# One more w1 block among the first transfers of a fused attention, soft MoE and FFN kernel

## The chip, the cores and the metric

The kernel runs on one core of one Trainium2 chip. The metric is the device time of one execution in microseconds (us), as a median of several runs; lower is better. One execution was also profiled.

## The reference

Three layers follow each other. All inputs and outputs are float32.

- Chunked attention over 4 batches, 8 heads, 768 positions and 64 dimensions: each chunk of 32 queries sees its own 32 keys, 16 to the left, 8 to the right and 8 memory keys.
- A soft mixture of experts on the 3072 tokens of width 512: 8 experts with 4 slots each. The logits `x @ phi` give one softmax over the tokens, which mixes the tokens into 32 slots, and one over the slots, which mixes the results back; between them each expert does `relu(slots @ w1[e]) @ w2[e]` with a hidden width of 1024.
- A feed-forward layer with a squared relu: `h = x @ w_in`, `g = s * relu(h)**2 + b`, `g @ w_out`, with a hidden width of 2048.

```python
x = attention(q, k, v, mem_k, mem_v)            # (3072, 512)
logits = x @ phi
d = softmax(logits, axis=0); slots = d.T @ x
slot_out[e] = relu(slots[e] @ w1[e]) @ w2[e]    # for 8 experts
x = softmax(logits, axis=1) @ slot_out
r = relu(x @ w_in); out = (s * r * r + b) @ w_out
```

## The kernel before

**The attention stage** works in 32 units. A unit is one pair of heads and one half (384 positions) of one batch. Four units make a group, of which there are eight; the group's tokens then go through the logits and the running softmax of the mixture. The loop at L488 is a software pipeline written out by hand: iteration s spreads K of unit s+1 on POOL (`kspread`), computes the scores of unit s on PE (`emit_s`, L291), does the softmax of unit s on DVE and ACT, transposes the probabilities of unit s-1 (`emit_t`, L323), multiplies those of unit s-2 by V (`emit_pv`, L331) and transposes the result of unit s-3 (`emit_xt`, L345). Steps of a finished group come in between.

**The transfers** are all issued on SP's queue, in the order of the program, and SP waits at each issue until its target buffer is free. `load_qk` (L246) brings Q and K of one unit, 396 KB, into one of five buffers. `load_v` (L256) brings V of two units, four transfers of 192 KB, into one of two buffers; it does so for even units only. `load_w(n)` (L189) brings the next n blocks of one list of weights: 16 blocks of w1, two of w_in, 16 of w2, then the rest. A block of w1 is 1 MB. A counter, `wnext`, remembers how far the list is; an argument `cap` makes a call do nothing once the counter has reached it. The first 15 blocks of w1 have places of their own, which nothing in the attention stage uses, so their issues wait for no engine. The sixteenth goes where attention had its keys, and later blocks go where keys, V or used blocks of w1 were.

Ahead of the loop a first set of transfers is issued (L457 to L465): K of unit 0, constants, K of units 1 and 2, one w1 block, V of units 0 and 1, K of unit 3, V of units 2 and 3, K of unit 4. In the loop each iteration s issues K of unit s+5 and, where s+1 is even and s is at least 3, V of units s+1 and s+2; every odd iteration ends with one w block, up to `NWA` = 15:

```python
            when(s + NKB, load_qk)
            if s >= 3:
                when(s + 1, load_v)
            if s % 2 == 1:
                load_w(1, NWA)
            if s == NU - 2:
                load_w(1)
        load_w(19 - wnext[0])
```

So the loop brings the fifteenth block in iteration 27, the sixteenth in iteration 30, and the call behind it three more.

**After attention** come eight steps with w1 (`emit_w1`, L655), sixteen with w2 (`emit_w2`, L696), and then the feed-forward layer (L881, L965, L977), whose weights come as halves of blocks (L203) as buffers come free. The last block of w2 is brought in three pieces (L212).

Of the kernel before, what the change touches and what calls it, by code (L numbers as in the profile page):

```python
# [34 lines left out]
def kernel(  # L35
# [54 lines left out]
    def area(pos, *shape, p=128):  # L90
        n = 1
        for d in shape:
            n *= d
        at, size, tile_ = next(x for x in segs if x[0] <= pos < x[0] + x[1])
        assert pos + n <= at + size
        a = tile_[0:p, pos - at:pos - at + n]
        if len(shape) == 2:
            a = a.rearrange("p (a b) -> p a b", a=shape[0])
        elif len(shape) == 3:
            a = a.rearrange("p (a b c) -> p a b c", a=shape[0], b=shape[1])  # L100
        return a
# [15 lines left out]
    with tc.manual_schedule():  # L117
# [71 lines left out]
        def load_w(n, cap=None):  # L189
            for _ in range(n):  # L190
                i = wnext[0]
                if i < (len(order) if cap is None else cap):
                    src = srcs[order[i][0]][order[i][1]]
                    p = at_[order[i]]
                    if p is SPLIT:
                        wt[order[i]] = [area(x, SLOT // 2) for x in p]
                        for x in range(2):
                            nc.sync.dma_start(out=wt[order[i]][x], in_=src[:, SLOT // 2 * x:SLOT // 2 * (x + 1)])
                        wnext[0] += 1
                        continue  # L200
                    if i >= npre:
                        t = area(p, SLOT // 2).bitcast(I32)
                        nc.sync.dma_start(out=t, in_=src.bitcast(I32)[:, SLOT // 2 * order[i][2]:SLOT // 2 * (order[i][2] + 1)])  # L203
                        wt[order[i]] = t
                        wnext[0] += 1
                        continue
                    t = area(p, SLOT)
                    if order[i] == ("w2", W2 - 1):
                        wt[order[i]] = [t[:, SLOT // 2 * x:SLOT // 2 * (x + 1)] for x in range(2)]
                        for x, w in ((0, 2), (2, 1), (3, 1)):  # L210
                            at = slice(SLOT // 4 * x, SLOT // 4 * (x + w))
                            nc.sync.dma_start(out=t[:, at], in_=src[:, at])  # L212
                        wnext[0] += 1
                        continue
                    if src.dtype != F32:
                        t, src = t.bitcast(I32), src.bitcast(I32)
                    nc.sync.dma_start(out=t, in_=src)
                    wt[order[i]] = t
                    wnext[0] += 1
# [19 lines left out]
        def unit(u):  # L239
            g, hp = divmod(u, NHP)  # L240
            b, hf = divmod(g, HALF)
            return g, b, hf, hp

        def load_qk(u):
            g, b, hf, hp = unit(u)
            nc.sync.dma_start(out=kbuf[(u + 3) % NKB][:, PAD:], in_=kq[b, hf, hp])  # L246

        def load_v(u):
            g, b, hf, hp = unit(u)
            if u % 2:  # L250
                return
            for h in range(2):
                for a in range(2):
                    r0 = 0 if a else LC - RC
                    src = vm[b, 2 * hp + h:2 * hp + 4:2, r0:r0 + CH, hf * NCU + a:hf * NCU + a + NCU, :]
                    nc.sync.dma_start(out=vbuf[u // 2 % 2][2 * h + a:128:4, :, h], in_=src.rearrange("x r c d -> r x (c d)"))  # L256
# [204 lines left out]
        load_w(1)  # L461
        load_v(0)
        load_qk(3)
        load_v(2)
        load_qk(4)  # L465

# [725 lines left out]
```

## Time and profile before

| what | us |
|---|---|
| median of 3 runs | 460.74 (460.23 to 462.44) |
| the profiled execution | 460.34 |
| its span, first to last instruction | 458.6 |
| PE busy in the span | 442.1 (96%) |
| ACT, DVE busy | 297.1 (65%), 283.9 (62%) |
| POOL busy | 84.8 (18%) |
| bytes by DMA | 83.03 MB, mean 181 GB/s |

PE is the TensorE matmul engine, DVE is VectorE, ACT is ScalarE, POOL is GpSimd and SP (SyncE) issues the transfers. A line such as L331 is a line of the kernel. Busy time of PE is modelled from pipelined matmuls, so a busy PE is not PE at its peak. The profile names who ended a wait from the semaphores' events.

### The profile page before, as it was taken

How to read it: one execution, taken by the hardware profiler on the slowest of the kernel's cores; microseconds unless marked ns; L12 is line 12 of the kernel's file. 1: busy time of each engine (PE TensorE's matmuls, PEld its weight loads, DVE VectorE, ACT ScalarE, POOL GpSimd, SP SyncE). 2: the span in 40 equal slices, each digit the busy share in tenths (PEclk: the TensorE clock that was granted, in tenths of full speed). 3: DMA queues.
4: the chain of work that ended last, by engine and by line, in shares of the span. 5: the costliest groups of instructions: out<-in, count | busy, mean ns of one | idle time of the engine just before them, and what ended most of it. 6: DMA issues, size and time to landing. Idle time of an engine off the chain costs nothing.

```text
span 458.6 us, 10105 instructions
## 1 busy us (share of the span) xinstructions
PE 442.1 (96%) x3936; PEld 339.8 (74%) x3936; DVE 283.9 (62%) x644; ACT 297.1 (65%) x588; POOL 84.8 (18%) x155
## 2 busy tenths in 40 slices
PE   6899999999999989999999999999999999999996
PEld 5666766667556468788787888888888888888885
DVE  5678888788674089698695958994722242224242
ACT  4566666666325199889797987666666666664660
POOL 6575555561000000000000000000870000000000
PEclk8899999999999999999999999999999999999999
DMA  8999999999999953245252100000500020002011
GB/s 305 370 407 409 403 407 406 400 391 377 417 417 418 407 212 105 94 138 185 91 187 90 46 1 0 1 1 0 218 13 1 1 91 1 0 2 91 0 70 69
DMA packets 22735, 83.03 MB, mean 181 GB/s; under 512 B 2976, under 2 KB 3104, under 8 KB 18592
## 3 DMA queue, kind: packets, MB, share of 16 engines
q1 hardware_dynamic: 22688, 82.39, 46.8%
q8 instruction: 31, 0.51, 0.5%
q14 instruction: 16, 0.13, 0.1%
HBM read 76.09 MB, written 6.29 MB: 180 GB/s over the span
## 4 chain that ended last, share of the span: by engine, by line
PE 80%; DMA 10%; DVE 4%; SPq 1%; issue 1%; ACT 1%; POOL 1%; DVEq 0%; POOLq 0%; ACTq 0%
PE g L965 13%; PE pt L965 6%; PE xt L965 6%; PE x L965 6%; PE lp L965 6%; PE g L977 6%; DMA vals<-in_vm_dram 6%; PE s L881 5%; PE lp L977 3%; PE xt L977 3%; PE pt L977 3%; PE x L977 3%; PE s L655 3%; PE x L331 3%; DMA keys<-in_w_out_dram 2%; PE s L291 2%
## 5 line engine op out<-in xcount | busy, mean ns | idle before, releaser
L916 DVE TENSOR_TENSOR glo<-keys,ghi 128x512 fp32r<-128x512 f32 x48 | 35.8, 751 | 60.0 <-ACT ghi L912 59.8
L904 ACT ACTIVATE keys<-s 128x512 f32<-128x512 f32 x48 | 28.7, 598 | 44.9 <-PE s L881 44.9
L916 DVE TENSOR_TENSOR glo<-r,ghi 128x384 fp32r<-128x384 f32 x64 | 35.3, 554 | 16.9 <-ACT ghi L912 16.6
L948 POOL TENSOR_TENSOR vals<-vals,bias 128x512 f32<-128x512 f32 x7 | 10.3, 1487 | 168.4 <-ACT keys L904 168.4
L307 ACT ACTIVATE seg<-seg 128x384 f32<-128x384 f32 x32 | 28.8, 901 | 18.2 <-DVE seg L318 14.8
L904 ACT ACTIVATE r<-s 128x384 f32<-128x384 f32 x64 | 31.1, 488 | 13.7 <-PE s L881 13.5
L977 PE MATMUL g<-wlo,ghi 128*128 128x512 f32 x128 | 39.6, 389 | 0.0
L965 PE MATMUL g<-whi,ghi 128*128 128x512 f32 x126 | 39.3, 390 | 0.0
L965 PE MATMUL g<-whi,glo 128*128 128x512 f32 x126 | 39.1, 389 | 0.0
L908 ACT ACTIVATE r<-r 128x384 f32<-128x384 f32 x63 | 33.2, 526 | 6.5 <-DVE glo L916 4.7
L881 PE MATMUL s<-cpack,mpack 128*128 128x384 f32 (+1 forms) x112 | 36.3, 360 | 0.0
L268 POOL TENSOR_SCALAR keys<-keys 64x416 f32<-64x416 f32 x63 | 33.6, 533 | 12.5 <-DMA keys<-in_kq_dram 7.7
L291 PE MATMUL s<-keys 128*32 128x128 f32 x768 | 29.6, 286 | 4.9 <-POOL keys L272 3.8
L912 ACT CAST ghi<-r 128x384 fp32r<-128x384 f32 x64 | 32.5, 508 | 1.9 <-PE g L977 0.4
L908 ACT ACTIVATE keys<-keys 128x512 f32<-128x512 f32 x48 | 30.4, 633 | 1.8 <-DVE glo L916 0.2
L331 PE MATMUL x<-vals,seg 128*32 128x128 f32 x744 | 28.9, 280 | 2.7 <-DMA vals<-in_vm_dram 2.4
L912 ACT CAST ghi<-keys 128x512 fp32r<-128x512 f32 x48 | 29.8, 621 | 1.6
L331 PEld LDWEIGHTS x<-vals,seg 128*32 128x32 f32 x744 | 21.0, 111 | 12.7 <-DVE seg L315 5.3
L325 ACT COPY seg<-pt 128x384 f32<-128x384 f32 x32 | 15.2, 476 | 19.4 <-PE pt L323 18.5
L977 PEld LDWEIGHTS g<-wlo,ghi 128*128 128x128 f32 x128 | 24.0, 188 | 5.0
L965 PEld LDWEIGHTS g<-whi,glo 128*128 128x128 f32 x126 | 23.7, 188 | 5.0
L291 PEld LDWEIGHTS s<-keys 128*32 128x32 f32 x768 | 19.1, 112 | 10.8 <-POOL keys L272 6.6
(291 smaller groups left out, 1052.2 us busy)
## 6 DMA issues: line engine op xcount, KB each, us to landing
seg<-in_w_dram SPq DMA_DIRECT2D x27, 1024.0 KB, 8.8
keys<-in_kq_dram SPq DMA_DIRECT2D x32, 396.0 KB, 7.4
vals<-in_vm_dram SPq DMA_DIRECT2D x64, 192.0 KB, 6.6
keys<-in_w_out_dram SPq DMA_DIRECT2D x16, 512.0 KB, 4.5
keys<-in_w_in_dram SPq DMA_DIRECT2D x10, 512.0 KB, 3.9
out_dram<-seg SPq DMA_DIRECT2D x18, 256.0 KB, 2.1
keys<-in_w_in_dram SPq DMA_DIRECT2D x2, 1024.0 KB, 8.1
vals<-in_w_dram SPq DMA_DIRECT2D x2, 1024.0 KB, 10.2
```

Of the source, the lines that this page charges most:

```text
L268: (nc.vector if h and u == 0 else nc.gpsimd).tensor_scalar(out=stream(kz[rows, h], 0, CH), in0=k[rows, UT * h:UT * h + (NCU + 1) * CH].rea ...
L291: nc.tensor.matmul(out=o, lhsT=qt[:, 32 * c:32 * c + 32], rhs=kz[:, :, at:at + WIN], start=True, stop=not (first or last))
L307: nc.scalar.activation(out=p_r[u], in_=sm_r[u].rearrange("p t h (a r) -> p t r (h a)", a=2), func=AF.Exp, scale=scale)
L325: nc.scalar.copy(out=pts_r[u], in_=pt)
L331: nc.tensor.matmul(out=xp[32 * r:32 * r + 32, t], lhsT=pts_r[u][:, 32 * c:32 * c + 32], rhs=vbuf[u // 2 % 2][:, u % 2, :, 64 * c:64 * c + ...
L881: nc.tensor.matmul(out=hq, lhsT=mpack[:, 128 * f:128 * f + 128], rhs=cpack[:, 128 * t0:128 * (t0 + nt)], start=True, stop=True)
L904: nc.scalar.activation(out=r_of(n), in_=h_t.pop(n), func=AF.Relu)
L908: nc.scalar.activation(out=r2_of(n), in_=r_of(n), func=AF.Square)
L912: nc.scalar.copy(out=g_of(n)[0], in_=r2_of(n))
L916: nc.vector.tensor_tensor(out=glo, in0=r2_of(n), in1=ghi.bitcast(F32), op=ALU.subtract)
L965: nc.tensor.matmul(out=o_t[r_][t], lhsT=g[x][:, 128 * t:128 * t + 128], rhs=w_hi[f], start=(first and x == 0), stop=False)
L977: nc.tensor.matmul(out=o, lhsT=ghi[:, 128 * t:128 * t + 128], rhs=w_lo[f], start=False, stop=(f == f1 - 1))
```

## The change

One call is added among the first transfers: the second block of w1 is issued after K of unit 3 and ahead of V of units 2 and 3.

```diff
@@ -461,6 +461,7 @@
         load_w(1)
         load_v(0)
         load_qk(3)
+        load_w(1)
         load_v(2)
         load_qk(4)
 
```

## Rows read from the trace of the kernel before

**Rows 1.** The page: the span, and the DMA engines' share in 40 slices, in tenths.
```profile
span 458.6 us, 10105 instructions
...
DMA  8999999999999953245252100000500020002011
```

**Rows 2.** Stretches: length, busy us (instructions) of PE, PEld, DVE, ACT, POOL; PEclk, DMA share, GB/s.
```profile
20.00:100.00 80.00, 76.39 (x1507) 52.98 (x1498) 65.93 (x196) 51.49 (x110) 50.46 (x108) 1.00 1.02 404
100.00:112.00 12.00, 11.80 (x245) 9.06 (x240) 10.54 (x35) 8.16 (x19) 2.97 (x7) 1.00 0.98 367
112.00:162.00 50.00, 48.20 (x688) 28.32 (x676) 22.66 (x70) 18.60 (x61) 1.25 (x4) 1.00 1.01 415
```

**Rows 3.** PE's groups by line, 20 to 100 us: count | busy, mean ns | idle before.
```profile
L331 PE MATMUL x<-vals,seg 128*32 128x128 f32 x594 | 22.4, 275 | 2.7 <-DMA vals<-in_vm_dram 2.4 <-DVE seg L315 0.2
```

**Rows 4.** PE's timeline, end of w2: start, us, what, count, [idle before <- releaser].
```profile
148.32 2.80 PE L696 MATMUL pt<-seg,seg 128*32 128x256 f32 x48
151.39 1.07 PE L696 MATMUL xt<-seg,seg 128*32 128x256 f32 x16 [0.28 <-DMA seg<-in_w_dram]
...
156.75 2.83 PE L696 MATMUL xt<-seg,seg 128*32 128x256 f32 x32
```

**Rows 5.** SP's issues, one by one: K of units 3, 4; V of unit 4 (last); w.
```profile
6.75 0.59 SPq L246 DMA_DIRECT2D keys<-in_kq_dram  x1
...
11.58 0.58 SPq L246 DMA_DIRECT2D keys<-in_kq_dram  x1
...
19.82 0.61 SPq L256 DMA_DIRECT2D vals<-in_vm_dram  x1
...
20.47 0.59 SPq L217 DMA_DIRECT2D seg<-in_w_dram  x1
```

**Rows 6.** SP's waits: total, times, longest; 0 to 15 us, then 102 to 106.
```profile
SPq L256 <- DMA seg<-in_w_dram: 1.6, 1, 1.6
...
SPq L256 <- PE g L439: 2.9, 1, 2.9
```

**Rows 7.** DMA issues of rows 5, same order: KB, us from issue to landing.
```profile
keys<-in_kq_dram SPq DMA_DIRECT2D x1, 396.0 KB, 6.5
...
keys<-in_kq_dram SPq DMA_DIRECT2D x1, 396.0 KB, 5.6
...
vals<-in_vm_dram SPq DMA_DIRECT2D x1, 192.0 KB, 6.8
...
seg<-in_w_dram SPq DMA_DIRECT2D x1, 1024.0 KB, 8.6
```

**Rows 8.** Stretches of 1 us, columns as in rows 2: 13 to 15 us.
```profile
13.00:14.00 1.00, 1.00 (x11) 0.63 (x11) 0.99 (x3) 0.02 (x1) 0.53 (x1) 0.50 0.90 291
14.00:15.00 1.00, 1.00 (x24) 0.87 (x24) 0.71 (x4) 0.75 (x2) 0.89 (x2) 0.50 0.83 277
```

**Rows 9.** Timeline: spread of K and scores of unit 4, V product of unit 4.
```profile
17.29 1.13 POOL L268 TENSOR_SCALAR keys<-keys 64x416 f32<-64x416 f32 x2 [1.72 <-DMA keys<-in_kq_dram]
...
19.50 0.86 PE L291 MATMUL s<-keys 128*32 128x128 f32 x24 [1.22 <-POOL keys L272]
...
26.71 1.09 PE L331 MATMUL x<-vals,seg 128*32 128x128 f32 x24 [0.65 <-DMA vals<-in_vm_dram]
```

**Rows 10.** Sixteenth w1 block: issue, landing; landing of a transfer issued alone at 169.53.
```profile
105.76 0.53 SPq L217 DMA_DIRECT2D keys<-in_w_dram  x1
...
keys<-in_w_dram SPq DMA_DIRECT2D x1, 1024.0 KB, 6.9
...
keys<-in_w_in_dram SPq DMA_DIRECT2D x1, 512.0 KB, 3.7
```

**Rows 11.** Stretches, columns as in rows 2: PE's early gaps and half clock.
```profile
5.01:9.16 4.15, 0.88 (x26) 0.64 (x26) 2.08 (x5) 0.86 (x1) 1.92 (x4) 0.90 1.00 393
9.16:15.00 5.84, 5.84 (x82) 4.20 (x82) 3.35 (x10) 2.12 (x4) 3.34 (x7) 0.50 0.97 362
```

## The prediction

> **What bounds the kernel now.** The page comes first: the line of DMA shares in 40 slices stands at nine or more from the second slice to the fourteenth and thins out after that [rows 1], so for a third of the span the transfers, not an engine, are the first suspect. The stretches view puts numbers on it: from 20 to 100 us the 16 DMA engines are busy all the time (share 1.02) and move 404 GB/s; from 112 to 162 us they move 415; between these lies a stretch of 12 us with 367 [rows 2]. PE is busy 76.39 of the 80 us from 20 to 100 us, so it is nearly full too, with 3.6 us of idle time. The groups of PE instructions by line show where most of that sits: the matmuls of L331 (probabilities by V) were idle for 2.7 us in sum, 2.4 of it put down to V transfers [rows 3]. So the attention stage runs at the pace of the transfers, with PE close behind.
>
> The other end of the stretch matters more. PE's timeline from 148 to 160 us shows the last blocks of w2: 16 matmuls start at 151.39 us after 0.28 us idle on a w transfer; the last 32 take 2.83 us where 48 took 2.80 just before, so they lose 2.83 - 1.87 = 0.96 us inside, and end at 159.58 [rows 4]. With no transfer late, PE would have been done 0.28 + 0.96 = 1.24 us earlier, at 158.34. Behind this comes the FFN, where the DMA share in the slices is a half and less [rows 1]; I take it to move as a block with the end of w2. So the time of the kernel follows the later of two things: the landing of the last w2 block, and PE's own work, which can be pushed back 1.24 us before it counts.
>
> **The change, part by part.** The added call takes the next block of a list, and a counter remembers where the list stands. It adds no transfer. The loop's own calls stop at a cap of 15 blocks, so every block up to that cap goes one call earlier, the fifteenth in the iteration of unit 25 rather than 27, and the call in the iteration of unit 27 finds the cap reached and issues nothing. One MB moves from there to the front; what comes from unit 30 on is the same list. No PE, DVE, ACT or POOL instruction is added.
>
> Cost on SP's queue: one more issue. The issues of K and V near it take 0.58 to 0.61 us [rows 5]. It stands before V of unit 2, which now waits on SP anyway: within the first 15 us SP sat 1.6 us on a w transfer in the midst of V of units 2 and 3 [rows 6]. So the issue is hidden there, I put it at nothing; without that cover it is 0.6 us, once.
>
> Price of the block in the transfer queue: 1.049 MB at 404 GB/s is 2.6 us [rows 2]. A block issued among others agrees: V of unit 4 ends at 19.82 + 6.8 = 26.6 us, the w block behind it at 20.47 + 8.6 = 29.1, 2.5 us later [rows 5, 7]. The Trainium skill, "DMA: Bandwidth & Descriptors", section "Where 436 GB/s comes from", says that for HBM to SBUF the HBM side binds, at about 358 GB/s; an estimate by that page is 2.9 us for the block and 0.3 us more at the end of the sum. The rows of this trace at 404 and 415 speak against it, and the measured rate is used.
>
> What is pushed back: K of unit 3 is issued before the block and lands at 6.75 + 6.5 = 13.25 us either way. Behind it come the block (2.6), V of units 2 and 3 (four of 192 KB, 0.49 each at 404 GB/s, 1.95) and K of unit 4 (396 KB, 1.0): 18.8 us, against 11.58 + 5.6 = 17.2 before [rows 5, 7]. That is 1.6 us later and not 2.6, since the block fills a hole: from 13 to 15 us the engines moved only 291 and 277 GB/s [rows 8], 0.6 us short of full rate. POOL starts to spread K of unit 4 as it lands, at 17.29, and PE waits 1.22 us for that and starts scores at 19.50 [rows 9]; now at 21.1. V of unit 4 is next: after 18.8 us K of units 5 and 6 (2.0), a w block (2.6), K of 7 and 8 (2.0) and V (1.95), 27.35 us against 26.6. PE's side: from 19.50 to 26.71 it worked all but the 0.65 us it waited for V [rows 9], so from 21.1 it reaches that point at 27.7, 1.0 us later than before. I call the delay that the attention loop carries from there c. Its bounds: 0.7 if V's landing decides, 2.6 if nothing at all is filled; the working gives 1.0 and the landing of K of unit 4 gives 1.6. I take c = 1.2, nearest to these two.
>
> From 30 us on the rate is full in both, the order within each pair of units is the same, so c is carried unchanged to the end of the loop. There the missing block gives it back to the transfers, but not to PE. V of units 30 and 31 is not late by bytes: SP waited 2.9 us for PE before it [rows 6], so it and the w block after it move with PE, by c. That block was issued at 105.76 and took 6.9 us, to 112.66, queued behind the block of unit 27 [rows 10]. Without queue it needs less: 512 KB alone took 3.7 us, of which 1.3 are bytes at 404 GB/s, so 2.4 + 2.6 = 5.0 us for 1 MB [rows 10]. It then lands at 110.8 + c, which is 1.9 - c = 0.7 us earlier than before, and all later blocks, w2 among them, follow at full rate, 0.7 us earlier.
>
> The sum: w2's transfers would allow the end of w2 at 159.58 - 0.7 = 158.9 us; PE's work, 158.34 + c, allows 159.5. The later one decides: 0.1 us earlier than before. The transfers finish sooner and PE has no time left to use it. The profiled execution took 460.34 us with a span of 458.6, so 460.2; the median of the runs shown is 0.4 us above that execution, and carried over to it the forecast is **460.6 us**: no change that can be told. About 0.5% (2.3 us) is what a measurement of this kernel can tell from none.
>
> **The rivals.** *The front has room for the block* (c near 0): the low rate from 13 to 15 us [rows 8] speaks for some room, but it is 0.6 us of 2.6. Then PE ends w2 at 158.3 us: 1.2 us saved, about 459.5. The chance is 0.15.
>
> *Nothing is filled*: the dip at 13 to 15 us is slow packets and not idle engines (the share there is still 0.90 and 0.83 [rows 8]). Then c = 2.6, PE ends w2 at 160.9, 1.4 us later: about 462.1. The chance is 0.12.
>
> *TensorE's clock falls once more*, the case on the slow side. Early in this run, after PE was busy for 0.88 us in the 4.15 from 5.01 to 9.16, the granted clock went to 0.50, that is 1.2 of 2.4 GHz, for all of the 5.84 us up to 15 [rows 11]; with the 0.90 of the stretch before, some 6.7 us at half clock, 3.3 us of PE's work. In the gap before unit 4's scores, 1.22 us, the clock stayed full [rows 2, 9]. The change makes that gap 1.22 + 1.6 = 2.8 us, in the middle of these. If it falls there, c becomes 1.2 + 3.3 = 4.5, PE ends w2 at 162.8, 3.3 us later: about 464.0, 0.7% slower. What decides is whether the loop makes up for it: PE has 3.6 us of idle time from 20 to 100 us [rows 2] and can catch up as long as V waits for PE's buffers no longer than the queue holds other work, which would cut the loss to 1 us or less. So the gap must bring the fall and the loop must fail to make it up: a chance of 0.09. The Trainium skill, "TensorE: Matmul & The Clock Gate", section "HAM oscillation — how this bites in real kernels", tells the same story of kernels whose matmuls wait for DMA: the clock falls in the wait and the next tile starts cold. By that rule the fall itself is likely here; the trace shows it once, and the price above is from its rows.
>
> **How the numbers follow.** The forecast's case has 0.64, the two cases beside it 0.15 and 0.12, the clock 0.09. The first three lie within 0.5% of the median; I leave 0.03 for a gain above that, out of the second case. So: faster 0.03, same 0.88, slower 0.09. The range takes in c from 0 to 2.6, 459.5 to 462.1, and a few tenths on either side for the scatter of runs (460.23 to 462.44 before): 459.3 to 462.6. It leaves out the clock's case.
>
> **What would show it.** Right: K of unit 3 still lands near 13.3 us, K of unit 4 near 18.8 and scores of unit 4 start near 21.1; the rate from 13 to 15 us is near 400 GB/s; the first V wait ends near 27.7; no w transfer is issued between V of unit 28 and V of unit 30, and the rate between 100 and 112 us has a deeper hole; PE's w1 stage starts some 1.2 us later; the wait before the 16 matmuls at 151.39 is gone, and the last 32 matmuls of w2 take under 2.3 us and end within 0.5 us of 159.58. Wrong: scores of unit 4 at 19.5 or at 22 us (c mis-sized), a granted clock of 0.50 after 18 us with the loop's end 3 us or more late, or last w2 matmuls that still wait for their transfer (then the end is the transfers' and not PE's).

## The result, and the profile after

The changed kernel took 463.37 us (median of 10 runs, 460.65 to 465.47) where the kernel before, in runs beside it, took 460.54 (458.41 to 462.44): a ratio of 1.0058, with an interval of 1.0040 to 1.0076. Measured once more, with the first experiment below, it was 463.08 against 460.90 us, 1.0044 (1.0028 to 1.0059). So it is slower, by about half a per cent: 2.2 to 2.8 us, where 460.6 and no change were forecast. The profiled execution of the changed kernel is the shortest of its ten, 460.65 us, and its rows answer to the steps of the prediction better than its total does.

The page and the stretches of the changed kernel (columns as in rows 2):

```profile
span 458.9 us, 10102 instructions
...
DMA  8999999998999963245252100000500020002011
```

```profile
20.00:100.00 80.00, 75.64 (x1491) 52.61 (x1491) 64.75 (x193) 50.48 (x107) 51.00 (x108) 1.00 1.02 405
100.00:112.00 12.00, 11.66 (x238) 8.82 (x237) 10.78 (x36) 7.88 (x17) 4.22 (x10) 1.00 0.84 305
112.00:162.00 50.00, 48.69 (x701) 29.09 (x700) 23.43 (x73) 19.39 (x62) 1.25 (x4) 1.00 1.01 410
13.00:14.00 1.00, 1.00 (x27) 0.83 (x27) 1.00 (x4) 0.48 (x1) 0.53 (x1) 1.00 0.99 410
14.00:15.00 1.00, 0.27 (x12) 0.00 (x0) 1.00 (x4) 0.43 (x1) 0.86 (x3) 1.00 0.94 368
...
104.00:108.00 4.00, 3.80 (x75) 2.52 (x65) 3.94 (x15) 2.42 (x6) 1.78 (x5) 1.00 0.62 193
```

The hole of [rows 8] is filled: 410 and 368 GB/s from 13 to 15 us, where it was 291 and 277. The price is at the tail: 305 GB/s from 100 to 112 us against 367 in [rows 2], and in the middle of that a stretch of 4 us with 193, where the kernel before moved 317. The bytes can be counted up. First the kernel before, then the changed one, in three stretches (from 20 to 104 us both move 403 GB/s):

```profile
0.00:20.00 20.00, 14.24 (x220) 10.94 (x224) 12.51 (x40) 9.33 (x10) 12.33 (x26) 0.83 0.89 329
104.00:116.00 12.00, 11.67 (x225) 8.47 (x217) 8.97 (x28) 7.40 (x18) 2.24 (x5) 1.00 0.98 380
116.00:157.00 41.00, 40.17 (x577) 23.71 (x577) 20.00 (x62) 15.04 (x48) 1.25 (x4) 1.00 1.01 415
...
0.00:20.00 20.00, 13.52 (x200) 10.38 (x200) 12.60 (x40) 9.35 (x10) 10.59 (x23) 1.00 0.92 348
104.00:116.00 12.00, 11.66 (x234) 8.86 (x227) 9.63 (x31) 7.50 (x18) 2.24 (x5) 1.00 0.85 302
116.00:157.00 41.00, 40.54 (x590) 24.07 (x582) 20.58 (x64) 15.32 (x50) 1.25 (x4) 1.00 1.01 416
```

The changed kernel is 0.38 MB ahead at 20 us, 0.9 us at 404 GB/s, and still is at 104 us. From 104 to 116 us it falls back by 0.94 MB, 2.3 us, and from there on both move at the same rate. So its transfers are 1.4 us behind for the rest of w1 and w2.

The issues on SP's queue and the DMA issues they belong to (KB, us to landing) of the changed kernel: the block, K of unit 4, and the sixteenth w1 block.

```profile
7.33 0.47 SPq L217 DMA_DIRECT2D seg<-in_w_dram  x1
...
12.29 0.58 SPq L246 DMA_DIRECT2D keys<-in_kq_dram  x1
...
106.97 0.53 SPq L217 DMA_DIRECT2D keys<-in_w_dram  x1
...
seg<-in_w_dram SPq DMA_DIRECT2D x1, 1024.0 KB, 8.9
...
keys<-in_kq_dram SPq DMA_DIRECT2D x1, 396.0 KB, 6.9
...
keys<-in_w_dram SPq DMA_DIRECT2D x1, 1024.0 KB, 6.8
```

PE's timeline of the changed kernel: scores and V product of unit 4, the first w1 step, the last w2 steps.

```profile
21.51 0.86 PE L291 MATMUL s<-keys 128*32 128x128 f32 x24 [3.18 <-POOL keys L272]
...
28.03 1.15 PE L331 MATMUL x<-vals,seg 128*32 128x128 f32 x24
...
122.01 3.23 PE L656 MATMUL s<-seg,keys 128*32 128x256 f32 x56
...
152.16 1.05 PE L697 MATMUL xt<-seg,seg 128*32 128x256 f32 x16
...
157.33 2.59 PE L697 MATMUL xt<-seg,seg 128*32 128x256 f32 x32
```

The same first w1 step in the kernel before:

```profile
120.79 3.66 PE L655 MATMUL s<-seg,keys 128*32 128x256 f32 x64
```

K of unit 4 lands at 12.29 + 6.9 = 19.2 us (17.2 in [rows 5, 7]), scores of unit 4 start at 21.51 (19.50 in [rows 9]) after a gap of 3.18 us, the V product of unit 4 starts at 28.03 (26.71), and the w1 stage 1.22 us later than before, which is the c = 1.2 of the prediction. The wait of 0.28 us before the 16 matmuls of [rows 4] is gone, and the last 32 matmuls of w2 end at 159.92, 0.34 us late. This execution is 0.31 us longer than the profiled one before. It could have been more: when the last piece of w2 landed, the kernel before had moved 62.77 MB (395 GB/s up to 158.91 us) and this one 62.43 (392 up to 159.26), so here 0.34 MB less, 0.8 us, of the transfers behind w2 had gone ahead of it. The usual execution loses seven to nine times as much, and the runs below ask where.

### The profile page after: what moved, and what is told of

Same layout as the page of the kernel before. It is cut to its first block, busy times and chain, and to the rows that moved or that the text cites. A ratio compares the mean times of both kernels' runs of the same rounds, so it can differ in the third digit from the quotient of the medians.

```text
span 458.9 us, 10102 instructions
## 1 busy us (share of the span) xinstructions
PE 441.3 (96%) x3936; PEld 339.6 (74%) x3936; DVE 284.0 (62%) x644; ACT 296.8 (65%) x588; POOL 84.9 (18%) x155
## 4 chain that ended last, share of the span: by engine, by line
PE 83%; DMA 6%; DVE 5%; ACT 1%; SPq 1%; issue 1%; POOL 1%; DVEq 0%; POOLq 0%; ACTq 0%
PE g L966 12%; PE pt L966 6%; PE xt L966 6%; PE x L966 6%; PE lp L966 6%; PE g L978 6%; PE s L882 5%; PE x L331 3%; PE lp L978 3%; PE xt L978 3%; PE pt L978 3%; PE x L978 3%; PE s L656 3%; DMA vals<-in_vm_dram 3%; PE s L291 2%; PE xt L697 2%
```

## The experiments

Four theories came up in turn. **Theory 1**: TensorE's clock falls in the longer gap ahead of unit 4's scores (a rival of the prediction). **Theory 2**, its first alternative: transfers alone delay the attention loop by more than PE's slack. **Theory 3**: the front is harmless, and the block that is missing at the tail leaves a hole in the transfers, which set the end of w2. **Theory 4**: what counts is c, the delay of PE at the end of the attention loop (read off below as the start of the w1 stage against 120.79 us), since SP issues K and V, and what stands behind them in its queue, only when PE has freed their buffers; the idle time of the transfers only shows where that happens to bite.

**The changed kernel again.** No edit.

> The changed kernel once more, unedited, for another profile and for the clock beside the time of each run. Theory 1 (TensorE's clock falls once more in the gap ahead of unit 4's scores, in most executions but not in the profiled one): about 1.006 of the kernel before; runs with more time at half clock are the longer ones; a profile that is 2 us or more longer shows matmuls of about twice the length after 18 us and the w1 stage starting 2 us or more after 122.0. Theory 2 (the transfers alone: the attention loop is delayed by more than the 1.24 us of slack in most executions): about 1.006 as well, but matmuls at full clock after 18 us in a long profile, and V's landings later than in the short one.

Measured: 463.08 us, 1.0044 (1.0028 to 1.0059); its profiled execution took 462.23. PE's timeline and one stretch of it:

```profile
21.61 1.38 PE L291 MATMUL s<-keys 128*32 128x128 f32 x24 [3.38 <-POOL keys L272]
...
122.58 2.80 PE L656 MATMUL s<-seg,keys 128*32 128x256 f32 x48
...
153.32 1.07 PE L697 MATMUL xt<-seg,seg 128*32 128x256 f32 x16 [0.41 <-DMA seg<-in_w_dram]
...
158.68 2.80 PE L697 MATMUL xt<-seg,seg 128*32 128x256 f32 x32
```

```profile
21.80:25.20 3.40, 3.40 (x53) 2.59 (x45) 1.27 (x4) 1.25 (x2) 2.93 (x7) 0.50 1.01 395
```

Here the clock did fall: it was granted at 0.50 from 21.8 to 25.2 us, behind the gap of 3.38 us, and the 24 score matmuls took 1.38 us where they took 0.86. c is 122.58 - 120.79 = 1.79 us. At the end, though, PE waits for w2's transfers again (0.41 us before the 16 matmuls), and the last matmuls end at 161.48: the transfers are late too.

**The gap filled with idle matmuls**, in the changed kernel and, as a control, in the kernel before (8 instead of 20):

```diff
+            if s == 4:
+                warm(20)
             when(s, emit_s)
```

> The changed kernel with 20 idle bf16 matmuls put into the gap of 3.18 us ahead of unit 4's scores (about 2.6 us of work at full clock, into a bank that nothing uses yet), so that PE is not idle there. Theory 1: the fall of the clock after 18 us goes away and with it most of the loss: 1.000 to 1.002 of the kernel before, some 460.5 to 461.5 us. Theory 2: the transfers are as they were, so 1.006 stays, or a little more where the added matmuls delay the scores.

> The control: the kernel before with 8 idle bf16 matmuls (about 1 us) in its own gap of 1.22 us ahead of unit 4's scores. Both theories: 1.000 of the kernel before within 0.2%, unless its own shorter gap costs the clock in some executions; then theory 1 gives a gain of up to 0.3%.

Measured: the changed kernel 463.08 us, 1.0041 (1.0023 to 1.0059); the control 460.13, 0.9986 (0.9970 to 1.0002). PE's timeline and clock of the first:

```profile
18.66 2.35 PE L477 MATMUL lp<-ident 128*128 128x256 bf16 x20
21.98 0.86 PE L291 MATMUL s<-keys 128*32 128x128 f32 x24 [0.97 <-POOL keys L272]
```

```profile
17.00:29.00 12.00, 11.03 (x215) 8.85 (x215) 7.49 (x20) 5.68 (x10) 7.99 (x17) 1.00 1.03 409
```

PE is busy through the gap and the clock stays full, and the loss is what it was, 1.0041 after 1.0044. So theory 1 falls as the cause of the loss, although the fall itself was seen; the intervals leave room for a small part. That profile, at full clock, took 463.12 us, with c = 2.0.

**The gap without the move.** The kernel before, with memsets on POOL ahead of the spread of unit 4's K:

```diff
+            if s == 3:
+                for i in (9, 10):
+                    nc.gpsimd.memset(area(i * SLOT, SLOT), 0.0)
             when(s + 1, kspread)
```

> The kernel before with no transfer moved, but with the gap: POOL does 3.5 us of memsets on two places for w1 blocks not yet loaded, ahead of the spread of K of unit 4, so that unit 4's scores start at about 21.3 us instead of 19.5. Theory 1: the clock falls after 18 us in many executions, slower by 0.2 to 0.6%, and less than the change where the loop makes up for it, since V still lands early. Theory 2: V and K land as before, so the loop catches up and the time stays within 0.1%.

Measured: 464.25 us, 1.0064 (1.0039 to 1.0089). The scores, the stretch behind them, and SP's wait in the total from 20 to 32 us:

```profile
21.53 0.86 PE L291 MATMUL s<-keys 128*32 128x128 f32 x24 [3.21 <-POOL keys L272]
...
20.00:40.00 20.00, 18.47 (x366) 13.91 (x370) 14.27 (x42) 11.59 (x24) 12.95 (x27) 0.91 0.96 344
...
SPq L246 <- PE s L296: 5.2, 2, 3.8
```

No transfer is moved and the loss is as large as the change's. Unit 4's scores are late, so K's buffers come free late: SP stands 5.2 us at K's issues, waiting for score matmuls (2.4 in the kernel before), and from 20 to 40 us the engines move 344 GB/s, not 407. Delaying PE delays the transfers. Theory 2 expected the loop to catch up within 0.1% and falls. In this profile the clock fell too, so how much of PE's delay is the gap and how much the clock is not told apart here; either way it is PE that was delayed, and no transfer was moved.

**Front alone, tail alone, and a hole elsewhere.** The block is early and the call of unit 1 is left out; the kernel before with the block of unit 27 issued at unit 13; the block is early and the call of unit 13 is left out:

```diff
-            if s % 2 == 1:
+            if s % 2 == 1 and s != 1:
                 load_w(1, NWA)
...
-                load_w(1, NWA)
+                load_w(2 if s == 13 else 1, NWA)
...
-            if s % 2 == 1:
+            if s % 2 == 1 and s != 13:
```

> The front of the change alone: the second w1 block stays ahead of V of units 2 and 3, and the w call in the iteration of unit 1 is left out, so that the fifteenth block comes in the iteration of unit 27 as in the kernel before. K of unit 4 is still late, and PE's gap ahead of unit 4's scores stays at about 3 us. Theory 3 (new: the end of w2 is set by its transfers, and these lose more in the hole behind V of unit 28, where no block is left to fill the wait for PE, than the front gains): 0.998 to 1.001 of the kernel before; the rate from 104 to 108 us is back near 320 GB/s and the sixteenth block lands no later than 112.9. Theory 1 (the gap and the clock): 1.003 to 1.006, since the gap is unchanged.

> The tail of the change alone: the front is that of the kernel before, and the block of the iteration of unit 27 is issued with that of unit 13 instead (two blocks there). PE's early gap is the short one. Theory 3: the block pushes V behind it by 2.5 us since nothing is idle there, and the hole behind V of unit 28 is as deep as in the change: 1.004 to 1.008, the rate from 104 to 108 us below 200 GB/s, the sixteenth block at 114 to 115.5. Theory 1: 1.000, as the clock stays full.

> The second block early as in the change, but it is the call in the iteration of unit 13 that is left out, so that the tail keeps its block at unit 27. Theory 3, if any idle time of the transfers counts alike: a hole of 1 to 2 us near 50 us in place of that at 104 to 108, 1.001 to 1.004; if the hole costs only because PE gates what comes behind it at the tail, 0.998 to 1.001 and the sixteenth block no later than 112.9. Theory 1: 1.003 to 1.006.

Measured, in this order: 463.45 us, 1.0052 (1.0029 to 1.0074); 464.08 us, 1.0066 (1.0042 to 1.0089); 461.87 us, 1.0021 (0.9993 to 1.0049). The front alone (scores, two stretches, SP's wait from 20 to 32 us):

```profile
22.48 1.50 PE L291 MATMUL s<-keys 128*32 128x128 f32 x24 [4.04 <-POOL keys L272]
...
20.00:40.00 20.00, 17.52 (x350) 13.21 (x351) 13.08 (x37) 10.47 (x21) 13.53 (x28) 0.91 0.91 328
104.00:108.00 4.00, 3.80 (x81) 2.94 (x75) 3.80 (x16) 2.85 (x10) 0.59 (x2) 1.00 1.03 397
...
SPq L246 <- PE s L296: 5.4, 2, 2.9
```

Theory 3 expected no loss with the tail whole. The tail is whole, 397 GB/s from 104 to 108 us, and the loss is there: the hole has moved to 20 to 40 us (328 GB/s), and SP waits 5.4 us for the scores. In the changed kernel the extra block covers that stretch (406 GB/s) and is missing 80 us later. The tail alone, whose early gap is 1.80 us, loses as much, with c = 3.6 us and 262 GB/s from 104 to 108 us: the two blocks at unit 13 stand ahead of V, and PE then waits 2.25 us for V.

```profile
69.00 1.51 PE L331 MATMUL x<-vals,seg 128*32 128x128 f32 x24 [2.25 <-DMA vals<-in_vm_dram]
...
104.00:108.00 4.00, 4.00 (x87) 3.26 (x87) 3.79 (x15) 2.98 (x8) 0.75 (x2) 1.00 0.67 262
```

In that profile the clock was at half behind both waits (a mean of 0.91 from 20 to 40 us and of 0.94 from 40 to 100), so not all of its c is the block's. The hole elsewhere is inconclusive: its interval holds both no change and the 1.0044 of the changed kernel, and its profile, c = 2.0, took 461.90 us.

**The front alone with idle matmuls**, the two edits above together:

> The front alone as in the run above it, with 20 idle bf16 matmuls in the gap ahead of unit 4's scores. Theory 3: 0.997 to 1.000, a little better than without them in those executions in which the clock would fall there. Theory 1: all of the loss of the front alone goes, from 1.003 to 1.006 down to 1.000.

Measured: 462.45 us, 1.0029 (1.0006 to 1.0052), against 1.0052 without them. The intervals overlap: some part of that loss may be the clock's, and most of it is not shown to be. In its profile the clock stayed full from 20 to 40 us (1.00), and c is still 2.5 us, against 2.65 with the fall.

**K of unit 4 first.** In the changed kernel, in the front alone, and in the kernel before (where there is no second block to pass); last, in the kernel before, K of unit 3 ahead of the first block as well:

```diff
         load_qk(3)
+        load_qk(4)
         load_w(1)
         load_v(2)
-        load_qk(4)
...
-        load_w(1)
-        load_v(0)
         load_qk(3)
-        load_v(2)
+        load_w(1)
+        load_v(0)
         load_qk(4)
+        load_v(2)
```

> The changed kernel with K of unit 4 issued ahead of the second w1 block (K of 3, K of 4, block, V of 2 and 3), so that PE's gap ahead of unit 4's scores goes, while V of units 2 and 4 stays late by the block. Theory 4 (new: the loop's delay at PE, c, sets when SP may issue all that is gated by PE's buffers, and the end of w2 follows c, wherever the transfers' idle time falls; what makes c is first of all the late K of unit 4): scores of unit 4 at 18 to 19 us, c of 0.5 to 1.3 from V of unit 4, 1.000 to 1.003 of the kernel before. Theory 3 (the missing block at the tail alone): 1.004 to 1.006, since the tail is that of the change.

> The same order of the first transfers, and the w call in the iteration of unit 1 left out, so that the tail keeps its block and V of unit 4 is not late. Theory 4: no gap and no late V, so c is 0 or below, 0.997 to 1.000, against the 1.005 of the front alone with K of unit 4 late. Theory 3: 0.998 to 1.001, as the tail is whole; the two differ in that theory 4 alone explains why the front alone was slow.

> The kernel before with K of unit 4 ahead of V of units 2 and 3, no block moved: K of unit 4 lands 2 us earlier and the gap of 1.22 us goes. Theory 4: PE is 1 us ahead until V of unit 4 holds it, c from -0.6 to 0: 0.998 to 1.000. Theory 3: 1.000.

> The kernel before with K of unit 3 ahead of the first w1 block and V, and K of unit 4 ahead of V of units 2 and 3: K of unit 3 lands at about 9 us, so that scores of unit 3 start near 14 instead of 15.6, and those of unit 4 near 17. Theory 4: c of -1 to -0.3, held by V of unit 4: 0.997 to 0.999. Theory 3: 1.000.

Measured: 462.54 us, 1.0040 (1.0025 to 1.0055); 459.98, 0.9991 (0.9973 to 1.0008); 460.43, 1.0004 (0.9987 to 1.0020); 460.34, 1.0002 (0.9986 to 1.0018). The first, PE's timeline:

```profile
18.58 0.86 PE L291 MATMUL s<-keys 128*32 128x128 f32 x24
...
20.40 0.86 PE L331 MATMUL x<-vals,seg 128*32 128x128 f32 x24 [0.43 <-DVE seg L315]
...
23.67 1.51 PE L291 MATMUL s<-keys 128*32 128x128 f32 x24 [1.93 <-POOL keys L272]
```

The gap only moves on: unit 4's scores are early, unit 5's wait 1.93 us for their K and run at half clock behind that (1.51 us for the 24), and c is 2.3 us. My number for this run was too good. The second, with the call of unit 1 left out (PE's timeline, then two stretches):

```profile
18.68 0.86 PE L291 MATMUL s<-keys 128*32 128x128 f32 x24
...
23.00 0.86 PE L291 MATMUL s<-keys 128*32 128x128 f32 x24 [1.67 <-POOL keys L272]
...
20.00:40.00 20.00, 18.33 (x383) 13.18 (x382) 16.36 (x48) 12.65 (x26) 13.13 (x28) 1.00 1.02 398
104.00:108.00 4.00, 4.00 (x74) 2.74 (x75) 3.79 (x11) 2.28 (x6) 2.08 (x5) 1.00 0.99 372
```

Unit 5's scores still wait, but the loop has caught up by unit 6: no hole is left in either stretch, c is -0.9 us, and the loss of 1.0052 is gone, by moving one transfer of 396 KB ahead of the block. That is theory 4; theory 3 expected no loss here either, but it expected none in the front alone, where it came. (This profile, 458.86 us, is one of the shortest of its twelve runs; at their median c will be nearer to 0.) It is no faster than the kernel before by more than the interval, and neither are the two orders without a second block. One of these, with K of unit 3 first, shows how little a fall of the clock can cost:

```profile
26.93:30.35 3.42, 3.42 (x51) 2.61 (x52) 1.02 (x2) 0.48 (x1) 1.28 (x3) 0.50 1.01 399
```

The clock was at half for 3.4 us, as in the changed kernel's longer profile, and yet c is 0.06 us and the execution took 460.28.

**Two more profiles of the changed kernel**, unedited.

> The changed kernel, unedited, once more for a profile: the two so far took 460.65 and 462.23 us, the median of the runs is near 463.3. Theory 4: an execution near 463 has c (the start of the w1 stage against 120.79 us) of 2 to 2.8, made before 40 us by later landings of the block, of K of unit 4 or of V of unit 4, or by half clock after 18 us, and w2's last landing is late by c within 1 us. Theory 3: c stays near 1.2 to 1.8 and the rest is lost by the transfers between V of unit 30 and the end of w2.

> The same kernel again, for a fourth profile; the same expectations as for the look above it.

Measured: 461.84 and 462.14 us, beside 460.37 for the kernel before. c is 1.89 us in both. In the first the clock was at 0.50 from 22.4 to 25.8 us; in the second it stayed full after 17.4 us, but K of unit 4 landed at 19.74 us and the scores started at 22.09:

```profile
22.40:25.80 3.40, 3.40 (x44) 2.27 (x42) 2.24 (x6) 1.51 (x3) 2.93 (x7) 0.50 1.04 404
...
22.09 0.86 PE L291 MATMUL s<-keys 128*32 128x128 f32 x24 [2.91 <-POOL keys L272]
```

From 104 to 116 us the three longer profiles of the changed kernel moved 283, 279 and 288 GB/s.

Over all 16 profiles the time follows c: the correlation of time and c is 0.96, and a line through them starts at 460.0 us for c = 0 and rises by 1.15 us for each us of c. The clock's column is the mean from 20 to 40 us; 0.91 means that it was at 0.50 for some 3.4 of the 20:

```
kernel                           c, us  clock  end of w2, us  time, us
before                            0.00   1.00      159.58      460.34
changed                           1.22   1.00      159.92      460.65
changed, again                    1.79   0.91      161.48      462.23
changed, first look               1.89   0.91      161.07      461.84
changed, second look              1.89   1.00      161.40      462.14
changed, idle matmuls             2.00   1.00      162.42      463.12
before, idle matmuls             -0.55   1.00      158.78      459.51
before, gap on POOL               2.68   0.91      161.89      462.62
front alone                       2.65   0.91      162.84      463.56
front alone, idle matmuls         2.46   1.00      161.67      462.39
tail alone                        3.59   0.91      163.86      464.62
hole elsewhere                    1.96   0.91      161.13      461.90
changed, K of unit 4 first        2.26   0.91      161.75      462.49
front alone, K of unit 4 first   -0.92   1.00      158.16      458.86
before, K of unit 4 first         1.21   1.00      160.66      461.41
before, K of units 3, 4 first     0.06   0.91      159.55      460.28
```

From the end of w2 to the end of the execution it is 300.70 to 300.77 us in all 16, and the last w2 matmul ends 0.67 us after the last w2 transfer has landed, in each of them. So the transfers do set the end of w2, as theory 3 had it; what falls is that the missing block at the tail is needed for the loss. In 13 of the 16 the sixteenth block is issued at 105.76 + c us, within 0.1: SP waits for PE just ahead of it, at V of unit 30, and what comes behind it queues up, the last piece of w2 for some 15 us from its issue to its landing.

The line alone does not tell cause from effect: in the tail alone late transfers delay PE first. That PE's delay is enough is shown by the gap on POOL, that its removal is enough by the front alone with K of unit 4 first. And c varies between executions of one kernel: the profile of the kernel before with K of unit 4 first has c = 1.21, though its runs show no loss (1.0004). One profile is not a kernel's c.

## Why the prediction was wrong

**What held.** The bound (transfers through the attention stage and w2, then a block that moves as one) held to 0.07 us. The way through the front held: K of unit 3 unmoved, the hole at 13 to 15 us filled, a gap ahead of unit 4's scores, then V of unit 4, and a delay c carried to the w1 stage (1.32 us at V of unit 4, 1.22 there). No w transfer went out between V of units 28 and 30, and the hole at the tail came.

**The step that failed** is the sum's "the later one decides", with its term "1.9 - c = 0.7 us earlier" for the transfers. I took PE's 1.24 us of waiting in w2 for slack that would absorb c, while the transfers finished sooner. The sixteenth block was to take 5.0 us from its issue without a queue. It took 6.8 (106.97 to 113.8) in the changed kernel's profile, as long as in [rows 10] with the queue, and landed 1.1 us later, not 0.7 earlier. While SP waited for PE to free V's buffer, now c later, the engines ran short of queued work (a share of 0.62 and 193 GB/s from 104 to 108 us); what was lost there is more than the front had gained, and behind it the transfers already ran at full rate and could not make it up. So they were 1.4 us behind from 116 us on, and 2.0 to 2.3 us in the three longer profiles by the same count. PE and the transfers moved back together, and the slack is still there at the end of w2: 0.41 us of waiting in the longer profile, as 0.28 in [rows 4], and the last 32 matmuls took 2.59 us even in the shortest one, where under 2.3 was forecast. The gap on POOL shows it without any block moved, and the front alone with K of unit 4 first shows the loss gone with c.

**The size of c** was 1.2 and is 1.22, 1.79, 1.89 and 1.89 in four profiles. K of unit 4 landed at 19.2 to 19.7 us instead of 18.8, and scores started at 21.5 to 22.1 instead of 21.1. The sum put K 1.6 us later, which counts 1.0 of the block's 2.6 us as filled, while the hole that it reads off [rows 8] is 0.6 us; with 0.6 it is 2.0 us and 19.2, as three of the four profiles have it. In two of the four the clock fell on top of that; there PE was 2.8 to 3.0 us late at V of unit 4 (29.54 and 29.66 against 26.71) and 1.8 to 1.9 at the w1 stage, so c was not carried unchanged: the loop made up about 1 us. The three longer executions are 1.5 to 1.9 us longer than the profiled one before.

**The rivals.** "The front has room" and "nothing is filled" priced c alone; the second, at c = 2.6 and 462.1 us, was nearer to the measured 463.1 to 463.4 than the forecast, by luck, since the hole was filled. The clock's rival came nearest with 464.0, and it had the right place: the granted clock fell behind the gap in two of four profiles. But it is not what makes the loss, since the loss was the same with PE kept busy there, so that nearness is luck too. The Trainium skill's rule of a clock that falls while matmuls wait for DMA ("TensorE: Matmul & The Clock Gate", "HAM oscillation — how this bites in real kernels") agrees with the two profiles in which it fell, after gaps of 3.38 and 3.06 us; in the other two, with gaps of 3.18 and 2.91 us, it did not. The Trainium skill's 358 GB/s for HBM to SBUF ("DMA: Bandwidth & Descriptors", "Where 436 GB/s comes from") is contradicted here as before: 405 and 410 GB/s over 80 and 50 us.

**The range** ended at 462.6, its upper end worked out with c = 2.6 of which PE's 1.24 us of slack took up about half. By the line through the profiles, drawn afterwards, c = 2.6 costs 3.0 us, an upper end of 463.7, which would have held the measured times.

**What stays open.** The profiles of the unedited changed kernel took 460.65 to 462.23 us, its runs up to 465.5. So even the usual execution, at 463.1 to 463.4, was not profiled; by the line it would have c = 2.7 to 3.0, which is argued and not shown. The tail's hole was never tried with c at 0, so what it would cost by itself, and how the changed kernel's loss divides between c and the missing block, is not known.

## What to carry to other kernels

Where transfers wait for buffers that an engine frees, engine and transfers are one loop: idle time that one of them shows near the end is no slack for a delay of the other, if that delay also holds up the transfers' issue. Here both were pushed back, by 1.15 us of time for each us of c. A block prefetched early delays what stands behind it in the queue; look for the first consumer that has no cover (here K of one unit, 396 KB), and let that pass first. A hole in the transfers that was filled at one place opened at another in these runs: at 104 to 108 us in the changed kernel, at 20 to 40 us in the front alone. Counting the bytes moved up to a few points in time, before against after, shows where it went.

## What was not expected of the hardware

The sixteenth block, 1 MB behind the last V transfers, took 6.8 us from issue to landing; 5.0 had been expected from 3.7 for 512 KB [rows 10]. V had all landed at 109.3 us, 2.6 us of bytes more is 111.9, and it landed at 113.8. The engines were not idle in between: from 109.31 to 113.75 us they moved 375 GB/s, 1.67 MB, so 0.6 MB of what was issued behind the block went ahead of its last bytes. Over the 16 profiles the block took 6.3 to 8.0 us. The granted clock fell to 0.50 in some executions of the same kernel and not in others, behind a gap of about the same length (3.38 and 3.18 us); in the tail alone it fell behind a gap of 1.80 us.
